# Low bits of the 64-bit weights moved from GpSimd and VectorE to ScalarE, and one VectorE product moved behind a state update

## The chip, the cores and the metric

The kernel runs on one core of a Trainium2 chip. The metric is device time in microseconds (us) of that core. The core's engines each work through a queue of their own in order: PE (TensorE, matmuls; PEld is its weight load), DVE (VectorE), ACT (ScalarE), POOL (GpSimd) and SP (SyncE, which issues the transfers here).

## The reference

Three stages follow each other: a chunked state-space attention, a dense feed-forward network, and a mixture of eight experts. Cut to what matters:

```python
# 1. attention: x (4,8,768,32), a (4,8,768), B and C (4,8,768,16), float32; chunks of 32
cum = cumsum(log(clip(a)))                       # per chunk
M   = (C @ B.T) * exp(cum_i - cum_j) * causal
y   = M @ x + (C @ state) * exp(cum)             # C times decay
state = exp(sum(la)) * state + B.T @ (x * exp(cum_last - cum))
# 2. dense: 3072 tokens, 256 -> 2048 -> 256; w_in and w_out are drawn as float64
h = x @ w_in;  x = maximum(0.01 * h, h) @ w_out
# 3. experts: argmax of x @ w_gate + modality_bias[modality_id], then
out[mask] = gate * (relu(x[mask] @ w1[e]) @ w2[e])
```

`w_in` and `w_out` reach the chip as 64-bit words (1,048,576 of them, two 32-bit halves each) and are turned into float32 there.

## The kernel before, in words

Tokens go in chunks of 128 (24 chunks; six to a batch row) and in six blocks of 512. Attention fills a block's four chunks into `xh` and `xl`, the high and low float32r parts of x. The dense stage then loops over 16 slices of d_ff for each block: `mm1(j, f)` makes `h` in six matmuls, ACT scales it (`sa`), DVE takes the maximum (`gg`), ACT rounds it (`gh`), DVE subtracts (`gl`), and `mm2(j, f)` uses `gh` and `gl` in six matmuls. Attention of the next block runs between these matmuls. Experts come last.

The first four chunks and the first four weight pieces run in an order written out by hand (`STAGED`, L981 to L997). Everything else is placed by the framework's planner, which simulates the run and puts an instruction into an engine's queue when its operands are ready by its own estimate; it may do so between two staged steps. Operations named in `pin` stay behind the engine's instruction that was traced before them; a manual dependency does so for one instruction.

The names that the change and the prediction touch:

- Weight pieces. Each of the 16 pieces (128x512 words) passes through `cv_hb`, `cv_lb`, `cv_or`, a rounding copy to `wih` or `woh` on ACT and a subtraction to `wil` or `wol` on POOL. `i0`, `i1`, `o0`, `o1` are the staged pieces; `hb` and `lb` have two buffers each; `raw` has three.
- `attn_cd(c)` makes `cd` = C times decay on DVE (not for the first chunk of a batch row, so not for 0, 6, 12, 18). `cd` has two buffers. `tr_d(c)` transposes it on PE and so frees its buffer; `tr_c(c)` makes `cm`.
- `p3_mm(c)` multiplies with the state `st` and fills `psy`; `p3_x(c)` evicts it into `xh` (ACT) and `xl` (DVE); `p3_st(c)` updates `st` on DVE. `mm1(0, 0)` needs `xl` of chunk 3.
- `attn_load(c)` issues four transfers on SP: `ct`, `bt`, `xt` and, from chunk 4 on, the broadcast `e` of 512 KB.

The staged end of chunk 3 reads: `(p3_mm, 3), (p3_x, 3), (orr, "o0"), (p3_st, 3), (cast, "o0"), (hb, "o1", 0, 1), (lb, "o1"), (sub, "o0"), (orr, "o1")`.

Of the kernel before, what the change touches and what calls it, by code (L numbers as in the profile page):

```python
# [11 lines left out]
I32 = mybir.dt.int32  # L12
U16 = mybir.dt.uint16
AF = mybir.ActivationFunctionType
ALU = mybir.AluOpType
# [2 lines left out]
PSUM = bass.MemoryType.PSUM  # L18
DRAM = bass.MemoryType.DRAM
NEG = -1.0e30  # L20
LOW, LOW0 = 0.9 * 2.0 ** -13, 0.2995
WHY = "the table is built on the chip from counts and clamped to this range"

# [65 lines left out]
def kernel(  # L89
# [70 lines left out]
    v, s, g, t_ = Pinned(nc.vector, "v"), Pinned(nc.scalar, "s"), Pinned(nc.gpsimd, "g"), Pinned(nc.tensor, "t")  # L160
# [49 lines left out]
    dfull = cst.tile([P, NB, NCB], F32, name="dfull")  # L210
    st = cst.tile([P, P], F32, name="st")
# [89 lines left out]
    dk = {}  # L301
# [62 lines left out]
    def attn_load(c, bcast=True):  # L364
# [10 lines left out]
            nc.sync.dma_start(out=e, in_=cumd[b * H:(b + 1) * H, sl].unsqueeze(0).to_broadcast([P, H, P]))  # L375
        ch[c] = dict(x=xt, b=bt, c=ct, e=e)

    def attn_mask(c):
        e = ch[c]["e"]
        r = g.affine_select(out=e, in_=e, pattern=[[0, H], [1, P]], compare_op=ALU.is_ge, fill=NEG, base=0, channel_multiplier=-1)  # L380
        if c == NC0:
            tc.add_manual_dep(
                r.ins, dk["last"].ins.name, mybir.DependencyInfo(mybir.DependencyClass.NoSync, mybir.DependencyReason.DATA),
                reason="behind the first chunks and conversions in the queue: it waits for a transfer",
            )

    def attn_cd(c):
        b, cc = divmod(c, NCB)
        if cc == 0:
            return  # L390
        d = ch[c]
        cd = ap_.tile([P, H, N], F32, tag="cd", name="cd")
        v.tensor_tensor(
            out=cd, in0=d["c"], in1=ecum[:, cc, b * H:(b + 1) * H].unsqueeze(2).to_broadcast([P, H, N]), op=ALU.mult
        )
        d["cd"] = cd

    def attn_exp(c, h0, h1, src=None):
# [141 lines left out]
    def p3_st(c):  # L540
        b, cc = divmod(c, NCB)
        ps = ch.pop(c)["psy"]
        if cc < NCB - 1:
            gmv = gm.rearrange("p (u a) d -> p u a d", a=2)
            bx = ps[:, 2 * P:2 * P + 64].rearrange("p (a d) -> p a d", a=2).unsqueeze(1).to_broadcast([P, 2, 2, D])
            pm = st if cc == 0 else ap_.tile([P, P], F32, tag="pm", name="pm")
            r = v.tensor_tensor(out=pm.rearrange("p (u a d) -> p u a d", u=2, a=2), in0=bx, in1=gmv, op=ALU.mult)
            readers.append(r)
            if cc > 0:
                v.scalar_tensor_tensor(out=st, in0=st, scalar=dfull[:, b, cc:cc + 1], in1=pm, op0=ALU.mult, op1=ALU.add)  # L550


    def split(raw, hi, lo, eng):
# [11 lines left out]

    def cv_lb(raw, hb, lb):
        w4 = raw.bitcast(U16).rearrange("p (f w) -> p f w", w=4)
        g.tensor_scalar(out=lb, in0=w4[:, :, 3], scalar1=32768.0, scalar2=-(2.0 ** 31), op0=ALU.is_ge, op1=ALU.mult)

    def cv_or(raw, hb, lb):  # L570
        w4 = raw.bitcast(U16).rearrange("p (f w) -> p f w", w=4)
        l2 = lb.bitcast(U16).rearrange("p (f w) -> p f w", w=2)
        v.tensor_scalar(out=l2[:, :, 0], in0=w4[:, :, 1], scalar1=LOW, scalar2=LOW0, op0=ALU.mult, op1=ALU.add)
        hi = hb.bitcast(I32)
        v.scalar_tensor_tensor(out=hi, in0=hi, scalar=3, in1=lb, op0=ALU.logical_shift_left, op1=ALU.bitwise_or)

    def to_f32(raw, q):
        c = cv_hb(raw)
        cv_lb(*c)
        cv_or(*c)  # L580
        return c[1]
# [348 lines left out]
    def p3(c):  # L930
        p3_mm(c)
        p3_x(c)
        p3_st(c)
# [7 lines left out]
    NC0 = blocks[0][1] // P  # L941
# [23 lines left out]
    def lb(key):  # L965
        if W64:
            cv_lb(*cvs[key][1])

    def orr(key):
        if W64:  # L970
            cv_or(*cvs[key][1])
# [5 lines left out]
    def sub(key):  # L977
# [3 lines left out]
    STAGED = [  # L981
        (decay_a,), (tr_mm, 0), (bc_mm, 0, 0), (bc_mm, 0, 1), (decay_b,), (tr_c, 0), (tr_b, 0), (decay_rows,),
        (bc_exp, 0, 0), (bc_mask, 0, 0), (bc_exp, 0, 1), (bc_mask, 0, 1), (cb_mm, 0), (decay_high,), (attn_cd, 1),
        (hb, "i0", 0, 0), (lb, "i0"), (decay_low_s,), (cb_bs, 0), (cb_mul, 0, 0), (cb_mul, 0, 1), (decay_low_v,),
        (cb_mul, 0, 2), (cb_mul, 0, 3), (decay_out,), (warm, 1, 6), (tr_mm, 1), (tr_d, 1), (tr_c, 1), (tr_b, 1), (tr_de, 1),
        (bc_mm, 1, 0), (bc_mm, 1, 1), (bc_exp, 1, 0), (bc_mask, 1, 0), (bc_exp, 1, 1), (bc_mask, 1, 1),
        (p3_mm, 0), (orr, "i0"), (p3_x, 0), (p3_st, 0), (decay_full_mm,), (decay_full,), (cb_mm, 1), (warm, 2, 4),
        (hb, "i1", 0, 1), (cast, "i0"), (cb_bs, 1), (cb_mul, 1, 0), (cb_mul, 1, 1), (attn_cd, 2), (cb_mul, 1, 2),
        (cb_mul, 1, 3), (lb, "i1"), (tr_mm, 2), (tr_d, 2), (tr_c, 2), (tr_b, 2), (tr_de, 2), (orr, "i1"), (attn_cd, 3),
        (bc_mm, 2, 0), (bc_mm, 2, 1), (bc_exp, 2, 0), (bc_mask, 2, 0), (bc_exp, 2, 1), (bc_mask, 2, 1),  # L990
        (p3_mm, 1), (p3_x, 1), (cast, "i1"), (sub, "i0"), (p3_st, 1), (cb_mm, 2), (cb_bs, 2),
        (cb_mul, 2, 0), (cb_mul, 2, 1), (cb_mul, 2, 2), (cb_mul, 2, 3), (tr_mm, 3), (tr_d, 3), (tr_c, 3), (tr_b, 3), (tr_de, 3),
        (bc_mm, 3, 0), (bc_mm, 3, 1), (bc_exp, 3, 0), (bc_mask, 3, 0), (bc_exp, 3, 1), (bc_mask, 3, 1),
# [28 lines left out]
    for c in range(NC0, NCH):  # L1022
        j, col = chunk_block(c)
        o = NF * (j - 1) + NF * col // blocks[j][1] + (Q["sh1"] if j == 1 else Q["sh"])
        if c > NC0 + 1:
            at(o - Q["ld"], attn_load, c)
        if col == 0:
            at(o - 1, new_xt, j)
        at(o - Q["cd"], attn_cd, c)
        at(o - Q["mk"], attn_mask, c)  # L1030
        at(o - Q["tr"], attn_tr, c)
        at(o - Q["ea"], attn_exp, c, 0, 4)
        at(o - Q["eb"], attn_exp, c, 4, 8)
        at(o - Q["c0"], attn_cb, c)
        at(o + Q["p3"], p3, c)
# [109 lines left out]
```

## Time and profile before

| | |
|---|---|
| median of 3 runs | 553.29 us (551.73 to 555.44) |
| profiled execution | 550.48 us, span 548.8 us |
| mean granted clock of PE | 0.967 |
| busy PE, DVE, ACT, POOL | 507.1, 350.2, 312.1, 196.9 us |

Times in the rows are counted from the start of the span. A granted clock of 1.00 is 2.4 GHz and 0.50 is 1.2 GHz. In timeline rows, brackets hold the idle time of the engine ahead of the instruction and what ended it. All helper calls have line L153, so tiles tell the rows apart.

### The profile page before, as it was taken

Reading aid. Unit: us, or ns where it says so; the run is one execution under the profiler, and the core shown is the slowest. Engines: PE = TensorE matmul, PEld = TensorE weight load, DVE = VectorE, ACT = ScalarE, POOL = GpSimd, SP = SyncE. Lnnn points to the kernel's source line nnn. Section 1 sums busy time; section 2 is a strip of 40 time slices with the busy share of each in tenths; the row PEclk is TensorE's granted clock in tenths of the full one; section 3 lists DMA queues with packets and bytes.
Section 4 is the critical chain, followed back from the end, with each engine's and each line's share of the span. In section 5 each row is a group of like instructions: output and inputs, shape, how many; then the busy total and the mean of one; then the engine's idle time right before and its main releaser. Section 6 shows DMA issues by size and latency. Waiting matters only on the chain.

```text
span 548.8 us, 9656 instructions
## 1 busy us (share of the span) xinstructions
PE 507.1 (92%) x3501; PEld 413.9 (75%) x3501; DVE 350.2 (64%) x729; ACT 312.1 (57%) x651; POOL 196.9 (36%) x167
## 2 busy tenths in 40 slices
PE   8857798899999999999999999999989999999991
PEld 5525476577777777677767877788879999999990
DVE  5746897866657675676657676766586665555640
ACT  5523868665555665565566646463536665566640
POOL 5557799310311012100310020073063456656331
PEclk9967989899999999999999999999989999999996
DMA  8895570431235221722060056642169767777400
GB/s 202 144 255 121 139 205 7 92 78 11 53 54 108 54 58 7 150 58 59 4 143 1 2 15 139 194 139 22 59 195 152 232 194 223 240 228 239 132 19 23
DMA packets 128311, 61.01 MB, mean 111 GB/s; under 512 B 84545, under 2 KB 120514, under 8 KB 128258
## 3 DMA queue, kind: packets, MB, share of 16 engines
q1 hardware_dynamic: 125186, 53.94, 42.4%
q0 software_dynamic: 3072, 6.41, 3.6%
q8 instruction: 29, 0.48, 0.4%
q14 instruction: 24, 0.20, 0.1%
HBM read 53.73 MB, written 6.60 MB: 110 GB/s over the span
## 4 chain that ended last, share of the span: by engine, by line
PE 58%; ACT 3%; issue 2%; DVE 2%; POOL 1%; POOLq 0%; DVEq 0%
PE y L153 16%; PE h L153 15%; PE hp L153 12%; PE o L153 10%; PE psy L153 2%; ACT e L153 1%; PE xps L153 1%; PE yr L153 1%; PE ps L153 1%; PE cb L153 1%; POOL out_dram L153 1%; DVE w2s L153 1%; ACT cdt L153 1%; PE lp L153 1%; DVE gg L153 0%
## 5 line engine op out<-in xcount | busy, mean ns | idle before, releaser
L153 ACT CAST gh<-gg 128x512 fp32r<-128x512 f32 x96 | 59.5, 620 | 73.4 <-DVE gg L153 72.0
L153 DVE TENSOR_TENSOR gl<-gg,gh 128x512 fp32r<-128x512 f32 x96 | 73.0, 761 | 32.7 <-ACT gh L153 31.3
L153 POOL TENSOR_SCALAR_AFFINE_SELECT e<-e 128x1024 f32<-128x1024 f32 (+1 forms) x28 | 29.1, 1045 | 171.0 <-DMA e<-cumd 55.9
L153 PE MATMUL h<-xh,wih 128*128 128x512 f32 x192 | 80.3, 423 | 6.6 <-DVE gg L153 5.0
L153 PE MATMUL h<-xl,wih 128*128 128x512 f32 x192 | 77.4, 403 | 5.6 <-DVE xl L153 5.6
L153 DVE TENSOR_TENSOR gg<-sa,h 128x512 f32<-128x512 f32 x96 | 65.6, 684 | 24.8 <-ACT sa L153 23.0
L153 PE MATMUL y<-gl,woh 128*128 128x512 f32 x192 | 76.7, 402 | 0.7 <-DVE gl L153 0.6
L153 PE MATMUL h<-xh,wil 128*128 128x512 f32 x192 | 76.2, 400 | 0.0
L153 ACT ACTIVATE sa<-h 128x512 f32<-128x512 f32 x96 | 56.9, 593 | 32.4 <-PE h L153 32.1
L153 PE MATMUL y<-gh,wol 128*128 128x512 f32 x192 | 75.0, 393 | 0.0
L153 PE MATMUL hp<-x2h,w1s 128*128 128x256 f32 x384 | 72.6, 285 | 0.0
L153 PE MATMUL o<-w2s,hh 128*128 128x256 f32 x384 | 69.3, 285 | 0.0
L153 PE MATMUL y<-gh,woh 128*128 128x512 f32 x192 | 66.7, 406 | 1.0 <-ACT gh L153 1.0
L153 DVE SCALAR_TENSOR_TENSOR hl<-hp,hh 128x512 fp32r<-128x512 f32 x48 | 33.0, 692 | 53.6 <-ACT hh L153 53.4
L153 PEld LDWEIGHTS hp<-x2h,w1s 128*128 128x128 f32 x384 | 61.8, 194 | 0.6
L153 PEld LDWEIGHTS o<-w2s,hh 128*128 128x128 f32 x384 | 58.4, 191 | 0.4 <-issue 0.4
L153 POOL TENSOR_TENSOR w2s<-r,w2s 128x1024 fp32r<-128x1024 f32 x12 | 33.4, 2785 | 65.4 <-ACT w2s L153 40.6
L153 PE MATMUL hp<-x2l,w1s 128*128 128x256 f32 x192 | 53.8, 286 | 0.0
L153 PEld LDWEIGHTS h<-xh,wih 128*128 128x128 f32 x192 | 36.7, 193 | 20.9 <-DVE gg L153 9.1
L153 ACT ACTIVATE hh<-hp 128x512 fp32r<-128x512 f32 x48 | 28.5, 597 | 40.6 <-PE hp L153 40.6
L153 ACT ACTIVATE e<-e,ncum 128x128 f32<-128x128 f32 x160 | 51.2, 395 | 0.0
L153 PE MATMUL o<-w2s,hl 128*128 128x256 f32 x192 | 51.1, 283 | 0.0
(192 smaller groups left out, 916.3 us busy)
## 6 DMA issues: line engine op xcount, KB each, us to landing
r<-in_moe_w_dram SPq DMA_DIRECT2D x48, 512.0 KB, 4.9
e<-cumd SPq DMA_DIRECT2D x20, 512.0 KB, 4.6
raw<-in_moe_w_in_dram SPq DMA_DIRECT2D x4, 1024.0 KB, 5.7
raw<-in_moe_w_out_dram SPq DMA_DIRECT2D x4, 1024.0 KB, 7.3
yx<-ysb SPq DMA_DIRECT2D x6, 528.0 KB, 3.3
xt<-in_x_dram SPq DMA_DIRECT2D x24, 128.0 KB, 4.4
ct<-in_C_dram SPq DMA_DIRECT2D x24, 64.0 KB, 3.1
bt<-in_B_dram SPq DMA_DIRECT2D x24, 64.0 KB, 2.7
```

The lines of the kernel that those rows point to most:

```text
L153: r = f(*args, **kw)
```

## The change

Two edits. First, the low 32-bit half: ScalarE now computes it (scale and bias on the low half's upper 16 bits, written as whole 32-bit words), where GpSimd wrote the sign bit as a word and VectorE then wrote the scaled low bits into that word's lower half. VectorE then joins in two steps: shift `hb` and or it with `lb`, as before; then take the sign bit from `raw` and or it in. No GpSimd instruction is left in `cv_lb`. Second, `cd` of chunk 4 (`NC0`) gets a manual dependency on the state update of the last staged chunk, 3, so that it stands behind it in DVE's queue.

```diff
+SIGN = -(2 ** 31)
...
+    def after(r, key):
+        tc.add_manual_dep(
+            r.ins, dk[key].ins.name, mybir.DependencyInfo(mybir.DependencyClass.NoSync, mybir.DependencyReason.DATA),
...
         if c == NC0:
+            after(r, "last")
...
     def attn_cd(c):
...
-        v.tensor_tensor(
+        r = v.tensor_tensor(
             out=cd, in0=d["c"], in1=ecum[:, cc, b * H:(b + 1) * H].unsqueeze(2).to_broadcast([P, H, N]), op=ALU.mult
         )
+        if c == NC0:
+            after(r, "lastv")
...
-                v.scalar_tensor_tensor(out=st, in0=st, scalar=dfull[:, b, cc:cc + 1], in1=pm, op0=ALU.mult, op1=ALU.add)
+                dk["lastv"] = v.scalar_tensor_tensor(out=st, in0=st, scalar=dfull[:, b, cc:cc + 1], in1=pm, op0=ALU.mult, op1=ALU.add)
...
     def cv_lb(raw, hb, lb):
         w4 = raw.bitcast(U16).rearrange("p (f w) -> p f w", w=4)
-        g.tensor_scalar(out=lb, in0=w4[:, :, 3], scalar1=32768.0, scalar2=-(2.0 ** 31), op0=ALU.is_ge, op1=ALU.mult)
+        s.activation(out=lb, in_=w4[:, :, 1], func=AF.Copy, scale=LOW, bias=LOW0)

     def cv_or(raw, hb, lb):
-        w4 = raw.bitcast(U16).rearrange("p (f w) -> p f w", w=4)
-        l2 = lb.bitcast(U16).rearrange("p (f w) -> p f w", w=2)
-        v.tensor_scalar(out=l2[:, :, 0], in0=w4[:, :, 1], scalar1=LOW, scalar2=LOW0, op0=ALU.mult, op1=ALU.add)
+        w = raw.bitcast(I32).rearrange("p (f w) -> p f w", w=2)
         hi = hb.bitcast(I32)
         v.scalar_tensor_tensor(out=hi, in0=hi, scalar=3, in1=lb, op0=ALU.logical_shift_left, op1=ALU.bitwise_or)
+        v.scalar_tensor_tensor(out=hi, in0=w[:, :, 1], scalar=SIGN, in1=hi, op0=ALU.bitwise_and, op1=ALU.bitwise_or)
```

The mask of chunk 4 kept its dependency on `last`; it now goes through the helper `after`.

## Rows read from the trace of the kernel before

**Rows 1.** Windows: span, PE, PEld, DVE, ACT, POOL busy, PEclk, DMA share, GB/s.

```profile
30.00:40.00 10.00, 6.11 (x63) 3.41 (x62) 4.27 (x11) 3.87 (x11) 7.16 (x6) 0.55 1.00 291
...
70.00:80.00 10.00, 9.99 (x54) 7.45 (x52) 10.00 (x20) 5.79 (x13) 9.62 (x6) 0.91 0.68 173
...
180.00:220.00 40.00, 40.00 (x251) 31.06 (x249) 26.07 (x62) 23.08 (x55) 6.42 (x6) 1.00 0.20 33
```

**Rows 2.** Timeline of PE at the first slice: start, duration, instruction, idle before.

```profile
38.22 1.22 PE L153 MATMUL h<-xh,wih 128*128 128x512 f32 x2 [0.51 <-ACT xh L153]
45.08 0.80 PE L153 MATMUL h<-xl,wih 128*128 128x512 f32 x1 [5.63 <-DVE xl L153]
```

**Rows 3.** Timeline of DVE, 24 to 51 us.

```profile
26.46 0.29 DVE L153 TENSOR_TENSOR cd<-ct,ecum 128x128 f32<-128x128 f32 x1 [2.36 <-DMA ct<-in_C_dram]
...
30.05 0.28 DVE L153 TENSOR_TENSOR cd<-ct,ecum 128x128 f32<-128x128 f32 x1
...
44.39 0.29 DVE L153 TENSOR_TENSOR cd<-ct,ecum 128x128 f32<-128x128 f32 x1 [8.12 <-DMA ct<-in_C_dram]
44.60 0.42 DVE L153 TENSOR_TENSOR xl<-psy,xh 128x256 fp32r<-128x256 f32 x1
...
48.24 0.69 DVE L153 TENSOR_TENSOR gg<-sa,h 128x512 f32<-128x512 f32 x1
49.62 1.06 DVE L153 TENSOR_TENSOR gl<-gg,gh 128x512 fp32r<-128x512 f32 x1 [0.69 <-ACT gh L153]
```

**Rows 4.** Timeline of PE: the transpose that reads chunk 4's `cd`.

```profile
35.31 0.42 PE L153 MATMUL ps<-ident,cd 128*128 128x128 f32 x1
```

**Rows 5.** Timeline of SP, 23 to 42 us.

```profile
23.50 0.38 SPq L371 DMA_DIRECT2D ct<-in_C_dram  x1
...
25.50 0.38 SPq L371 DMA_DIRECT2D ct<-in_C_dram  x1
...
29.60 7.59 SPq L375 DMA_DIRECT2D e<-cumd  x3
...
40.82 1.57 SPq L371 DMA_DIRECT2D ct<-in_C_dram  x1
```

**Rows 6.** Groups by shape, 13 to 110 us: busy, mean ns, idle before, releasers.

```profile
L153 POOL TENSOR_SCALAR lb<-raw 128x512 int32<-128x512 uint16 x16 | 33.3, 2080 | 6.0 <-DVE hb L153 6.0
L153 DVE SCALAR_TENSOR_TENSOR hb<-hb,lb 128x512 int32<-128x512 int32 x16 | 12.9, 807 | 2.6 <-ACT hb L153 2.2
L153 ACT ACTIVATE hb<-raw 128x512 f32<-128x512 f32 x16 | 10.8, 678 | 0.0
L153 DVE TENSOR_SCALAR lb<-raw 128x512 uint16<-128x512 uint16 x16 | 9.2, 572 | 0.0
```

**Rows 7.** Waits between 24 and 110 us: total, times, longest.

```profile
PE h L153 <- DVE gg L153: 4.8, 4, 2.4
...
PEld psy L153 <- POOL lb L153: 1.3, 1, 1.3
```

**Rows 8.** Timeline of ACT ahead of the longest of those waits.

```profile
66.50 0.65 ACT L153 ACTIVATE hb<-raw 128x512 f32<-128x512 f32 x1
67.04 0.59 ACT L153 ACTIVATE sa<-h 128x512 f32<-128x512 f32 x1
```

**Rows 9.** Timeline of POOL and DVE where they run side by side.

```profile
56.97 1.29 POOL L153 TENSOR_TENSOR wil<-hb,wih 128x512 fp32r<-128x512 f32 x1
57.43 1.37 DVE L153 SCALAR_TENSOR_TENSOR hb<-hb,lb 128x512 int32<-128x512 int32 x1
...
81.97 2.38 POOL L153 TENSOR_SCALAR lb<-raw 128x512 int32<-128x512 uint16 x1
...
83.46 0.69 DVE L153 SCALAR_TENSOR_TENSOR hb<-hb,lb 128x512 int32<-128x512 int32 x1
```

**Rows 10.** Timeline of ACT and DVE around the first piece.

```profile
13.99 0.62 ACT L153 CAST cumb<-cr 64x512 bf16<-64x512 f32 x1 [0.17 <-DVE cr L153]
...
15.38 0.68 DVE L153 TENSOR_TENSOR cumb<-cr,cumb 32x512 bf16<-32x512 f32 x1
```

More of the change, by code (lines that the diff above doesn't have):

```diff
@@ L376, in attn_load @@
         ch[c] = dict(x=xt, b=bt, c=ct, e=e)
+    def after(r, key):
+        tc.add_manual_dep(
+            r.ins, dk[key].ins.name, mybir.DependencyInfo(mybir.DependencyClass.NoSync, mybir.DependencyReason.DATA),
+            reason="behind the first chunks in the queue: it waits for a transfer",
+        )
     def attn_mask(c):
@@ L381, in attn_mask @@
         if c == NC0:
[L382 to L385, printed above, removed]
+            after(r, "last")
     def attn_cd(c):
```

## The prediction

> **What bounds the kernel now.** I read the windows first. In the middle of the span PE has no idle time at all: 40.00 of 40.00 us between 180 and 220, at the full clock [rows 1]. Time can be won only where PE waits, and the change touches nothing behind some 105 us. So I looked at the start, and there the window from 30 to 40 us stands out: PE is busy 6.11 of 10 us, and its granted clock is 0.55, so even its busy time is mostly at the 1.2 GHz level. VectorE and ScalarE are idle for more than half of it, while the DMA share is 1.00 [rows 1].
>
> The PE timeline names the loss. The first two matmuls of the dense stage run at 38.22, the third follows after 5.63 us of idle time that `xl` ended [rows 2]. The DVE timeline says why: `xl` stands right behind a `cd` that waited 8.12 us for a `ct` transfer. An earlier `cd` waited 2.36 us for the same kind of transfer [rows 3]; in the staged order `xl` and the state update of chunk 1 come next.
>
> Which chunks are these? The timeline doesn't say, so I counted. `cd` is not made for chunk 6, and the three before 26 us are those of chunks 1 to 3, by their place in the staged order. So 26.46 is chunk 4, 30.05 is chunk 5, and the long wait at 44.39 is chunk **7**, not the chunk that the change moves. It could stand there only because a buffer was free: there are two, and PE read chunk 4's at 35.31 [rows 4], before chunk 7's product was made.
>
> **The change part by part: the moved product.** Behind chunk 3's state update, chunk 4's `cd` can no longer hold `xl` of chunk 1; up to 2.36 us go there. What matters more: chunk 7's `cd` needs the buffer that chunk 4's frees, so it now also comes behind that update, and thus behind `xl` of chunk 3. The edit removes both waits from ahead of the first slice.
>
> What is late next? Chunk 7's `ct` itself. It is issued at 40.82, behind three broadcast loads that keep SP for 7.59 us [rows 5] while the DMA share is 1.00 [rows 1]. The change takes nothing out of that queue, so I leave the arrival at 44.39. The question is what stands behind chunk 7's `cd` when DVE reaches it. PE can transpose chunk 4's product only after it is made, so the earliest place is about when the first `gg` is made. The first free stretch on DVE there is the 0.69 us in which `gl` waits for `gh` [rows 3], and a product whose operands the planner takes as landed fits in. Then DVE waits until 44.39, works 0.29, and the first `gl` starts at 44.68 in place of 49.62: **4.9 us** earlier. The matmuls of two slices, the joins of `o0` and `o1`, and the first `gg` lie in the time that was idle.
>
> The bounds: if the product is put ahead of the second join and of `gg`, these run behind it, 44.68 + 2 x 0.69 + 0.69 + 0.69 = 47.44, and 2.2 us are left. If it comes so late that the transfer has landed, the slice starts at 38.22 - 2.36 = 35.86; from `xl` at 44.60 to `gl` at 49.62 it took 5.02; with 0.4 for the eviction and 0.24 for the longer join `gl` starts at 41.5, a gain of 8.1.
>
> **The low bits.** GpSimd loses 16 x 2.08 = 33.3 us [rows 6]. I price this at nothing: in that group it was GpSimd that waited for VectorE, 6.0 us. One weight load of PE, 1.3 us, is put down to `lb` [rows 7]; it loads a product of chunk 3's `e`, which `lb` doesn't write, so I take that for a wait on VectorE's `e`, and the bound for what goes with it is those 1.3 us.
>
> ScalarE gains 16 instructions. Nothing in the trace reads 16-bit words into a word on ScalarE; the nearest row is `hb`, the same strided source and the same 512 results, 0.678 [rows 6]. Three pieces come before 46 us and fall beside idle time. The tightest is the first: the added instruction pushes the low-part copy at 13.99 by some 0.54, but that ended at 14.61 and was used only at 15.38 [rows 10]; the cover is 0.77, and past it the whole first chunk chain would move. Of the 13 others, all could be hidden (0), or each could push the next instruction by the 0.54 that lie between the starts of `hb` and `sa` at 66.50 [rows 8]: 7.0 us. PE waits four times for `gg`, 4.8 us in all [rows 7], and the longest of these follows that very pair. I take two of thirteen as seen: **1.1 us**.
>
> VectorE trades a 0.572 step for a second join. It has two inputs like the first, one of them strided, so I price it by the first: 0.807 on average, 0.235 more [rows 6], 3.1 us for 13 pieces. The bounds are 0 and that. From 70 to 80 us DVE was busy 10.00 and PE 9.99 [rows 1]: both full, so some of it must show. I take a third: **1.0 us**. The raw tile is also held until the second join, by at most two joins, 1.6 us; SP's next weight load starts that much later. I charge nothing: no wait for a weight load was among those that held PE.
>
> Does GpSimd's absence speed VectorE up? A join beside a GpSimd subtraction took 1.37, but one that ran inside a GpSimd `lb` took 0.69, as if alone [rows 9]. The Trainium skill, page SBUF — State Buffer, section Who interferes with whom, says that a VectorE instruction with two SBUF inputs contends with a GpSimd instruction that reads SBUF and that the loser blocks for the whole instruction. The subtraction's rows agree with it, `lb`'s row does not; by the page the joins would get faster and the sum 0.6 better.
>
> Sum: -4.9 + 1.1 + 1.0 = **-2.8 us**. Against the profiled execution's own 550.48 us that is 547.7. It lies 2.8 below the median of the runs shown, 553.29, and outside their spread, so the prediction is made against the median: **550.5 us**, 0.5% faster.
>
> **The rivals.**
> - The wait goes altogether: chunk 7's product is placed past 44.39. For it: nothing forces it early, and DVE has much queued there. Against: it was placed as early as its buffer allowed before. -8.1 + 2.1 = -6.0: 547.3.
> - The wait moves and keeps its price: chunk 7's product stands ahead of the second join and of `gg`. -2.2 + 2.1: 553.2.
> - The edit doesn't do what it says at chunk 1: chunk 5's `cd` takes chunk 4's old place. Its `ct` is issued 2.0 us later [rows 5], so the wait would grow by 2.0 and all that follows with it. The slice then starts at 40.2 and `gl` at 45.9, a gain of 3.8 less 2.1: 551.6. Against it: in the trace chunk 5's came only 3.6 us later, at a place of its own.
> - Slower: **ScalarE becomes the bound**. It must give `sa` and `gh` in every slice, and 13 more instructions arrive in the same 58 us. From the point where it has no idle time left ahead of `sa`, every one delays a slice: 7.0, and 3.1 of VectorE in full, less 4.9, is +5.2: 558.5. For it: rows 8. Against it: ScalarE was busy only 5.79 of 10 us from 70 to 80 [rows 1].
> - VectorE is freed from GpSimd: the joins fall from 0.807 to 0.69, 1.9 us over 16; a third of it shows: 549.9. This is the page's rule; the row inside `lb` speaks against it.
>
> **How the numbers follow.** Forecast 35%; wait gone 25%; wait moved 17%; chunk 5 in the old place 8%; ScalarE the bound 10%; VectorE freed 5%. About 1% (5.5 us) is what a measurement of this kernel can tell from no change. Faster by more than that, below 547.8, are most of the second case and the lower edge of the first: 0.28. Slower by more, above 558.8, is somewhat under half of the ScalarE case and a planner's order that I don't foresee: 0.08. The rest is 0.64. The range goes from the wait gone with no added cost, 553.29 - 8.1 = 545.2, to the wait that kept its price with half of ScalarE's 7.0 and all of VectorE's 3.1: 553.29 - 2.2 + 6.6 = 557.7.
>
> **What the profile will show.** Right: no `cd` ahead of `xl` of chunks 1 and 3; the 5.63 us of PE gone; a DVE wait for `ct` that still ends near 44.4, with `gl` right behind it; ACT's `lb` near 0.68 and the second join near 0.69 to 0.81; PE waits for `gg` between 50 and 105 us grown by about two. Wrong: the DVE wait ends with another instruction behind it than I say, or is not there; the waits for `gg` grow by more than five; or blocks after 105 us take another time than before, since the planner orders the whole kernel anew.

## The result and the profile after

The changed kernel takes 560.41 us (median of 4 runs, 558.10 to 562.12) beside 552.51 for the kernel before on the same chip: ratio 1.0126, 95% interval 1.0085 to 1.0168. Slower, and outside the predicted range of 545.2 to 557.7. The profiled execution took 559.24, span 557.3, granted clock 0.961.

PE is busy as long as before, 507.4 us against 507.1, so 8.2 of the 8.5 us of longer span are idle time of PE. The windows of the changed kernel show where (span, PE, PEld, DVE, ACT, POOL, PEclk, DMA share, GB/s; they answer to [rows 1]):

```profile
30.00:40.00 10.00, 1.09 (x2) 0.37 (x2) 0.00 (x0) 0.00 (x0) 2.65 (x3) 0.50 1.04 275
...
70.00:80.00 10.00, 7.33 (x43) 4.74 (x43) 6.97 (x18) 8.30 (x18) 4.15 (x5) 1.00 0.49 121
180.00:220.00 40.00, 40.00 (x254) 30.48 (x253) 28.80 (x69) 23.79 (x57) 7.20 (x7) 1.00 0.31 60
```

From 30 to 40 us the core all but stands still: PE is busy 1.09 of 10 us, GpSimd 2.65, DVE and ACT not at all, while the transfers run. The middle of the kernel is full, as before. Summed over windows, PE is idle 6.8 us ahead of 30 us (before 7.0), 13.2 from 30 to 48 (before 9.0), 11.8 from 48 to 110 (before 8.9) and 3.0 from 110 to 360 (before 2.0).

The timeline of PE in the changed kernel, which answers to [rows 2]:

```profile
43.74 1.08 PE L154 MATMUL psy<-e,xt 128*32 128x128 f32 x16 [12.65 <-DVE e L154]
...
45.55 1.22 PE L154 MATMUL h<-xh,wih 128*128 128x512 f32 x2 [0.51 <-ACT xh L154]
46.57 0.63 PE L154 MATMUL h<-xl,wih 128*128 128x512 f32 x1
```

The 5.63 us ahead of the `xl` matmul are gone, as forecast. But PE now waits 12.65 us, and not in the dense stage: it waits for chunk 3's `e`, one step of the attention earlier. The timeline of DVE (answers to [rows 3]):

```profile
28.74 0.42 DVE L154 TENSOR_TENSOR xl<-psy,xh 128x256 fp32r<-128x256 f32 x1 [2.16 <-ACT xh L154]
40.74 1.34 DVE L154 TENSOR_TENSOR bs<-bt,e 128x128 f32<-128x128 f32 x1 [10.99 <-POOL e L154]
45.53 0.42 DVE L154 TENSOR_TENSOR xl<-psy,xh 128x256 fp32r<-128x256 f32 x1 [1.93 <-ACT xh L154]
47.78 0.28 DVE L154 TENSOR_TENSOR cd<-ct,ecum 128x128 f32<-128x128 f32 x1
...
51.17 0.28 DVE L154 TENSOR_TENSOR cd<-ct,ecum 128x128 f32<-128x128 f32 x1
51.37 0.68 DVE L154 TENSOR_TENSOR gl<-gg,gh 128x512 fp32r<-128x512 f32 x1
```

No `cd` waits for `ct` any more. DVE waits 10.99 us for a mask from GpSimd, chunk 3's, and the first `gl` starts at 51.37 in place of 49.62. A mask (`AFFINE_SELECT`) overwrites the part of a chunk's `e` on one side of the diagonal; it stands between the making of `e` and its use. Chunks 0 to 3 get their `e` from ACT, the later ones from a broadcast transfer. So the next view is GpSimd's timeline:

```profile
36.58 1.09 POOL L154 TENSOR_SCALAR_AFFINE_SELECT e<-e 128x1024 f32<-128x1024 f32 x1 [12.21 <-DMA e<-cumd]
38.44 2.26 POOL L154 TENSOR_SCALAR_AFFINE_SELECT e<-e 128x1024 f32<-128x1024 f32 x3 [0.76 <-DMA e<-cumd]
40.67 1.26 POOL L154 TENSOR_TENSOR wil<-hb,wih 128x512 fp32r<-128x512 f32 x1
```

GpSimd waited 12.21 us for a broadcast transfer before it masked a chunk with it. That first mask is 128x1024, a whole chunk; a staged chunk is masked in two instructions of 128x512. The second row groups three masks of two shapes. Which chunks? The order of GpSimd's instructions in the built program tells them by buffer number (`e_197` is chunk 2's, `e_204` chunk 3's; `e_613`, `e_680`, `e_862` are those of chunks 5, 6, 7). Before, and then changed:

```
AFFINE_SELECT e_197<-e_197 128x512 x2
TENSOR_TENSOR wil_138<-hb_313,wih_137 128x512
AFFINE_SELECT e_204<-e_204 128x512 x2
...
AFFINE_SELECT e_613<-e_613 128x1024

AFFINE_SELECT e_197<-e_197 128x512 x2
TENSOR_TENSOR wil_138<-hb_313,wih_137 128x512
AFFINE_SELECT e_613<-e_613 128x1024
AFFINE_SELECT e_680<-e_680 128x1024
AFFINE_SELECT e_204<-e_204 128x512 x2
```

The planner put the masks of chunks 5 and 6 ahead of chunk 3's last two. Chunk 4's mask has a manual dependency on `last`; those of 5 and 6 have none. GpSimd ran them in that order: chunk 3's masks, whose operand came from ACT, which had no work from 30 to 40 us, waited behind two that needed a 512 KB transfer each. One wait has gone out of DVE's queue, and another, longer one stands in GpSimd's. The waits between 24 and 110 us (total, times, longest) show it passed on, and answer to [rows 7]:

```profile
POOL e L154 <- DMA e<-cumd: 19.8, 5, 12.2
...
PE psy L154 <- DVE e L154: 12.7, 1, 12.7
DVE bs L154 <- POOL e L154: 11.0, 1, 11.0
...
PE h L154 <- DVE gg L154: 6.4, 4, 3.0
DVE hb L154 <- ACT lb L154: 5.8, 5, 3.0
```

The groups by shape, 13 to 110 us (busy, mean ns, idle before and its releaser), answer to [rows 6]; the two joins are told apart by their operands, `hb<-hb,lb` the first and `hb<-raw,hb` the second:

```profile
L154 DVE SCALAR_TENSOR_TENSOR hb<-raw,hb 128x512 int32<-128x512 int32 x16 | 13.4, 839 | 0.2
L154 DVE SCALAR_TENSOR_TENSOR hb<-hb,lb 128x512 int32<-128x512 int32 x16 | 11.6, 725 | 5.8 <-ACT lb L154 5.8
...
L154 ACT ACTIVATE lb<-raw 128x512 int32<-128x512 uint16 x15 | 9.9, 672 | 0.0
```

### The profile page after: what moved, and what is told of

Same layout as the page of the kernel before. It is cut to its first block, busy times and chain, and to the rows that moved or that the text cites. A ratio compares the mean times of both kernels' runs of the same rounds, so it can differ in the third digit from the quotient of the medians.

```text
span 557.3 us, 9643 instructions
## 1 busy us (share of the span) xinstructions
PE 507.4 (91%) x3501; PEld 412.6 (74%) x3501; DVE 350.3 (63%) x729; ACT 320.5 (58%) x667; POOL 165.7 (30%) x151
## 4 chain that ended last, share of the span: by engine, by line
PE 73%; DVE 9%; ACT 7%; issue 4%; DMA 2%; POOL 2%; SPq 1%; POOLq 0%; DVEq 0%; ACTq 0%
PE y L154 21%; PE h L154 21%; PE hp L154 11%; PE o L154 10%; PE psy L154 4%; ACT e L154 2%; DVE hb L154 2%; PE cb L154 2%; DMA e<-cumd 1%; PE ps L154 1%; DVE e L154 1%; PE yr L154 1%; ACT lb L154 1%; DVE gg L154 1%; PE xps L154 1%
```

## The experiments

Theory (the "queue theory" of the expectations): the loss is the order of GpSimd's queue. Rivals: the moved product makes it; ScalarE's added work makes it; GpSimd, emptied, let the masks forward; the second join costs by itself. Each run is compared with the kernel before on the same chip.

**e1: hold the masks of chunks 5 to 7 behind chunk 3's.** All of the change stays.

```diff
         if c == NC0:
             after(r, "last")
+        elif c < NC0 + 4:
+            after(r, "lastm")
...
-        g.affine_select(
+        dk["lastm"] = g.affine_select(
```

> The changed kernel with one more hold: the masks of chunks 5 to 7 stand behind the last staged mask of chunk 3 in GpSimd's queue. Queue theory (most of the loss is the GpSimd queue, where two masks that wait for transfers stand ahead of chunk 3's mask): GpSimd no longer waits ahead of chunk 3's mask, the first slice starts near 36 us in place of 45.6, the first gl near 44.7 to 46 in place of 51.4, and the time falls by 4 to 6 us, to 554 to 556. ScalarE theory (the loss is the 16 added ScalarE instructions): the time stays at 559 to 561, and PE waits for gh, gl and gg after 48 us stay. Moved-product theory (the new place of chunk 4's product is itself the loss): stays at 559 to 561.

Measured: 553.15 us, ratio 1.0025 (0.9999 to 1.0051). Of the loss, 7.3 us come back by the medians, 5.6 by the ratios; the queue theory said 4 to 6. In the built program GpSimd's queue is the only one that differs from the changed kernel's, and only in where those masks stand. DVE's timeline:

```profile
37.47 0.42 DVE L154 TENSOR_TENSOR xl<-psy,xh 128x256 fp32r<-128x256 f32 x1 [1.94 <-ACT xh L154]
...
43.79 1.30 DVE L154 TENSOR_TENSOR cd<-ct,ecum 128x128 f32<-128x128 f32 x1
45.01 0.68 DVE L154 TENSOR_TENSOR gl<-gg,gh 128x512 fp32r<-128x512 f32 x1
```

`xl` of chunk 3 starts 8.1 us earlier than in the changed kernel and the first `gl` 6.4. The wait in GpSimd's queue is the main cause. But `gl` is also 4.6 earlier than before the change, and yet the time is that of before: something gives it back later. Up to ACT's copy of the sixth dense block's result, where both have run the same 2312 matmuls, PE was idle 25.6 us in e1 and 26.7 before, and busy 367.0 and 364.6.

**e2: the moved product alone**, on the kernel before, bits untouched.

```diff
-        v.tensor_tensor(
+        r = v.tensor_tensor(
             out=cd, in0=d["c"], in1=ecum[:, cc, b * H:(b + 1) * H].unsqueeze(2).to_broadcast([P, H, N]), op=ALU.mult
         )
+        if c == NC0:
+            tc.add_manual_dep(
+                r.ins, dk["lastv"].ins.name, mybir.DependencyInfo(mybir.DependencyClass.NoSync, mybir.DependencyReason.DATA),
...
-                v.scalar_tensor_tensor(out=st, in0=st, scalar=dfull[:, b, cc:cc + 1], in1=pm, op0=ALU.mult, op1=ALU.add)
+                dk["lastv"] = v.scalar_tensor_tensor(out=st, in0=st, scalar=dfull[:, b, cc:cc + 1], in1=pm, op0=ALU.mult, op1=ALU.add)
```

> The kernel before with the moved product alone; the low bits stay on GpSimd and VectorE. Queue theory: GpSimd's order is that of the kernel before, so there is no wait there; both VectorE waits ahead of xl go; 2.2 to 8.1 us faster than before by the bounds of the prediction, 545 to 551, and the first gl at 44.7 to 47.4. ScalarE theory: the same, since nothing is added to ScalarE. Moved-product theory: slower than before, 556 to 561.

Measured: 549.76, ratio 0.9955 (0.9930 to 0.9980). DVE's timeline:

```profile
36.68 0.43 DVE L153 TENSOR_TENSOR xl<-psy,xh 128x256 fp32r<-128x256 f32 x1 [1.93 <-ACT xh L153]
...
43.56 1.09 DVE L153 TENSOR_TENSOR gl<-gg,gh 128x512 fp32r<-128x512 f32 x1 [0.69 <-ACT gh L153]
44.58 0.71 DVE L153 TENSOR_TENSOR cd<-ct,ecum 128x128 f32<-128x128 f32 x1
```

The moved product is a gain, so the rival that blames it falls. `gl` starts 6.1 us earlier than in [rows 3], and chunk 7's `cd` stands behind it with nothing to wait for. Only some 2.5 of the 6.1 reach the end; the busy times of its profile show one reason:

```profile
PE 510.1 (93%) x3501; PEld 414.5 (76%) x3501; DVE 354.3 (65%) x729; ACT 312.2 (57%) x651; POOL 196.0 (36%) x167
```

The span of this execution is 548.0, so PE is idle 37.9 us in place of 41.7; but the same 3501 matmuls are busy 3.0 us longer. The windows of e2 show more work where the granted clock is low:

```profile
30.00:48.00 18.00, 14.09 (x70) 9.26 (x67) 13.86 (x24) 7.17 (x16) 13.50 (x11) 0.65 0.96 219
```

Before, PE was busy 9.04 us in that stretch, at a clock of 0.53. A mean of 0.65 is part 1.2 and part 2.4 GHz, and PE had been waiting ahead of it. Matmuls moved there from later stretches at nearly full clock are busy longer; that the 3.0 us come from them is how I read it and wasn't tried by itself. It is a reading of one execution of each kernel: over all runs beside e2 the median granted clock was 0.960 before and 0.967 in e2, the other way round than in these two (0.967 and 0.962). So why 2.5 us and not 6.1 reach the median stays open in part. From 48 to 110 us PE is idle 10.0 us in place of 8.9.

**e3: the bits alone** (the changed kernel without the dependency of chunk 4's `cd`).

```diff
-        if c == NC0:
-            after(r, "lastv")
```

> The changed kernel without the hold on chunk 4's product. Queue theory: the wait on GpSimd stays, and VectorE waits for ct ahead of xl come back as well, partly beside it: 559 to 563. ScalarE theory: the added instructions cost the same as in the changed kernel: 559 to 561. Moved-product theory: back to the kernel before, 552 to 554.

Measured: 558.34, ratio 1.0109 (1.0061 to 1.0157). GpSimd waits 8.2 us for the broadcast and DVE 5.7 for GpSimd. The loss belongs to the edit of the bits; beside its wait, the moved product makes no difference that can be told (1.0109 without it, 1.0126 with it).

**e4: the low bits on GpSimd**, as whole words, the two joins kept.

```diff
-        s.activation(out=lb, in_=w4[:, :, 1], func=AF.Copy, scale=LOW, bias=LOW0)
+        g.tensor_scalar(out=lb, in0=w4[:, :, 1], scalar1=LOW, scalar2=LOW0, op0=ALU.mult, op1=ALU.add)
```

> The changed kernel with the low bits as whole words on GpSimd in place of ScalarE; the two joins on VectorE and the moved product stay. The masks of chunks 5 and 6 still stand ahead of chunk 3's in its queue. Queue theory: the first slice still starts near 45 us; with the ScalarE part (about 3 us of PE waits after 48 us) gone the time is 556 to 559, and with none of it gone 559 to 561. ScalarE theory (all of the loss): 552 to 554.

Measured: 557.93, ratio 1.0105 (1.0061 to 1.0150). GpSimd has its 16 instructions again and ScalarE none of the added ones, yet the masks of chunks 5 and 6 stand ahead as in the changed kernel: GpSimd waits 8.9 us, DVE 7.6. So neither the emptied GpSimd nor ScalarE turns the order over. What is left that e3, e4 and the changed kernel share is the pair of joins.

**f1: e1 with the low bits on GpSimd** (the edit of e4 on e1).

> As e1 (masks of chunks 5 to 7 behind chunk 3's, moved product, two joins), but the low bits are made by GpSimd as whole words (multiply and add, 0.97 us each in e4) and not by ScalarE (0.66 each in e1). It takes 16 of some 0.66 us from ScalarE and leaves the second join. If ScalarE's added work is what puts e1 (553.15) behind the product alone (549.76): 549 to 550.5, and the waits of TensorE for gh in the weight stretch gone back. If it is the second join on VectorE: about 553, as e1, with TensorE's wait for gg at 7 us or so. If GpSimd's own time at 48 to 60 us decides (11.69 of 12 us busy with the product alone): under 549.

Measured: 555.73, ratio 1.0062 (1.0040 to 1.0084). The ScalarE theory wanted 549 to 550.5; f1 is 2.0 us slower than e1 by the ratios, 2.6 by the medians, and outside all three expectations. In DVE's timeline chunk 7's `cd`, which stands ahead of the first `gl` in e1 too, waits again:

```profile
34.75 0.42 DVE L154 TENSOR_TENSOR xl<-psy,xh 128x256 fp32r<-128x256 f32 x1 [1.93 <-ACT xh L154]
...
44.79 0.29 DVE L154 TENSOR_TENSOR cd<-ct,ecum 128x128 f32<-128x128 f32 x1 [3.22 <-DMA ct<-in_C_dram]
45.00 1.77 DVE L154 TENSOR_TENSOR gl<-gg,gh 128x512 fp32r<-128x512 f32 x1
```

`xl` of chunk 3 is 2.7 us earlier here than in e1, and the wait uses that lead up: the first `gl` starts when e1's does. So the wait doesn't set f1 apart from e1. The profile is also of the fastest of the seven runs (553.08). The reason wasn't found.

**f2: an idle ScalarE activation for each piece**, on e2, masks held; its result is read by nothing.

```diff
+        idle = ap_.tile([P, 512], I32, tag="idle", name="idle")
+        s.activation(out=idle, in_=w4[:, :, 1], func=AF.Copy, scale=LOW, bias=LOW0)
```

> The product alone, with the low bits on GpSimd as before and one join, and for each of the 16 pieces one more ScalarE activation of the same size whose result nobody reads (16 of some 0.66 us). If ScalarE's added work is what e1 loses against the product alone: about 553. If it isn't: 549.5 to 550.3, as the product alone (549.76).

Measured: 551.90, ratio 0.9991 (0.9964 to 1.0017), 2.1 over e2, between what the two theories said. Twelve of the activations between 48 and 110 us took 0.674 us each. This is what the added work costs if nothing is taken away elsewhere.

**f3 and f3b: a second join for each piece**, on e2, masks held; the 16-bit step stays, the sign is set twice. The same kernel ran twice; the rows below are of the second run.

```diff
         v.scalar_tensor_tensor(out=hi, in0=hi, scalar=3, in1=lb, op0=ALU.logical_shift_left, op1=ALU.bitwise_or)
+        v.scalar_tensor_tensor(out=hi, in0=w[:, :, 1], scalar=-(2 ** 31), in1=hi, op0=ALU.bitwise_and, op1=ALU.bitwise_or)
```

> The product alone, with the low bits on GpSimd as before, and for each of the 16 pieces a second join on VectorE that sets the sign bit once more (16 of some 0.7 us). If the second join is what e1 loses against the product alone: 552 to 553.5, with TensorE's wait for gg longer than with the product alone. If it isn't: 549.5 to 550.3.

> The kernel of f3 once more, for a profile at the clock of the other runs. If the second join is what costs: again 556 to 559, with VectorE busier between 48 and 110 us than with the product alone and TensorE idle there for 14 us or more, against 10.0. If f3's time came from something else: nearer 550, or the idle time in another stretch.

Measured: 558.49, ratio 1.0096 (1.0060 to 1.0133), and 558.86, ratio 1.0132 (1.0090 to 1.0174): 7.8 to 9.8 us over e2 by the ratios. That is three times what the join theory said for f3 (2.2 to 3.7 over e2); f3b's expectation, written after f3, came true. The windows from 48 to 110 us, f3b first, then e2:

```profile
48.00:110.00 62.00, 47.72 (x251) 32.68 (x252) 59.31 (x97) 40.51 (x95) 48.04 (x28) 0.91 0.41 105
```

```profile
48.00:110.00 62.00, 51.99 (x292) 35.10 (x292) 53.69 (x96) 44.45 (x108) 46.71 (x29) 0.92 0.46 118
```

With the join, DVE is busy 59.31 of 62 us, all but full, and PE is idle 14.3 against 10.0.

**g1: the sign word as a float times zero on GpSimd**, on e2, masks held; one join.

```diff
-        g.tensor_scalar(out=lb, in0=w4[:, :, 3], scalar1=32768.0, scalar2=-(2.0 ** 31), op0=ALU.is_ge, op1=ALU.mult)
+        g.tensor_scalar(out=lb.bitcast(F32), in0=w[:, :, 1], scalar1=0.0, scalar2=None, op0=ALU.mult)
```

> The product alone with the masks held, and GpSimd's sign word made by one multiplication (upper word as a float times zero, which leaves only the sign) in place of the comparison and multiplication of 2.08 us. One join, the 16-bit step and ScalarE as in the kernel before. If the form of the operation sets GpSimd's time, as the low bits of e4 (0.97) say, the sign word takes about 1.0 us and GpSimd is no longer full from 48 to 60 us: 546 to 548.5, and the idle time of TensorE from 48 to 110 us under the 10.0 of the product alone. If GpSimd's fullness was not on the path: 549.5 to 550.

Measured: 550.44 beside 553.19, ratio 0.9946 (0.9917 to 0.9975); e2 had 0.9955, so no difference that can be told. The sign word took 1.70 us, not 1.0, and PE was idle 10.2 us from 48 to 110. A miss: this form of the sign word isn't the fast one that was expected, and whether GpSimd's fullness is on the path stays open.

**g2: the sign word by ScalarE**, as times zero with -0.0 added, on e2, masks held; one join, the 16-bit step on DVE. The weights came out without their sign, so the experts get other tokens, with more blocks of work (3601 weight loads in place of 3501). The time at the end, 575.66 (ratio 1.0431, 1.0389 to 1.0473), tells nothing; up to the last dense block the work is the same in kind and count.

```diff
-        g.tensor_scalar(out=lb, in0=w4[:, :, 3], scalar1=32768.0, scalar2=-(2.0 ** 31), op0=ALU.is_ge, op1=ALU.mult)
+        s.activation(out=lb.bitcast(F32), in_=w[:, :, 1], func=AF.Copy, scale=0.0, bias=-0.0)
```

> The product alone with the masks held, and the sign word by ScalarE (upper word as a float times zero), nothing by GpSimd: ScalarE's 16 added activations and GpSimd's emptied queue as in e1, but one join and the 16-bit step in place of two joins. If the second join is what holds e1 back (553.15): 547 to 549.5. If ScalarE's added work is: 552 to 553, as e1 and the idle activation (551.9).

Measured by ACT's copy of the sixth dense block's result: 390.71 us, against 392.55 in e1 and 389.22 in e2. These are single executions, 1.8 and 1.5 us apart, which is too little to decide; it leans to the join as what holds e1 back.

**h1: the changed kernel without its second join**, nothing held. It leaves the sign of the weights out, so again only the time up to the sixth block counts (at the end 574.13, ratio 1.0404, 1.0336 to 1.0471, from two runs, 575.90 and 572.36; the profile is of the first).

```diff
         v.scalar_tensor_tensor(out=hi, in0=hi, scalar=3, in1=lb, op0=ALU.logical_shift_left, op1=ALU.bitwise_or)
-        v.scalar_tensor_tensor(out=hi, in0=w[:, :, 1], scalar=SIGN, in1=hi, op0=ALU.bitwise_and, op1=ALU.bitwise_or)
```

> The changed kernel without its second join and with nothing else: the sign of the weights is left out, so the experts get other tokens and the time behind some 390 us can't be compared; what counts is the time up to the last copy of a dense block's result. In every program built so far with two joins a piece, the planner puts the masks of chunks 5 and 6 ahead of chunk 3's last staged masks on GpSimd; in those with one join it puts them behind, and so in this one. If the second join is what turns the order over: no wait of GpSimd near 12 us, the split of chunk 3 on VectorE near 37 us in place of 45.53, the first gl near 45 in place of 51.37, and the sixth block's first copy near 391 in place of 399.48. If the emptied GpSimd queue or ScalarE's work makes the loss: GpSimd's wait and 399 stay.

Measured. GpSimd's timeline, and DVE's:

```profile
27.99 1.22 POOL L154 TENSOR_SCALAR_AFFINE_SELECT e<-e 128x512 f32<-128x512 f32 x2 [3.64 <-ACT e L154]
...
39.96 1.34 POOL L154 TENSOR_SCALAR_AFFINE_SELECT e<-e 128x1024 f32<-128x1024 f32 x1 [9.52 <-DMA e<-cumd]
```

```profile
34.24 0.42 DVE L154 TENSOR_TENSOR xl<-psy,xh 128x256 fp32r<-128x256 f32 x1 [1.93 <-ACT xh L154]
...
39.65 0.69 DVE L154 TENSOR_TENSOR gl<-gg,gh 128x512 fp32r<-128x512 f32 x1 [0.69 <-ACT gh L154]
45.33 0.82 DVE L154 TENSOR_TENSOR cd<-ct,ecum 128x128 f32<-128x128 f32 x1 [4.98 <-DMA ct<-in_C_dram]
```

Chunk 3's two masks run at 27.99, ahead of the broadcast masks. GpSimd still waits 9.52 us for a transfer, but behind them, where chunk 3 doesn't need it. With the second join goes the order, though GpSimd is as empty and ScalarE as loaded as in the changed kernel. ACT's copies of the sixth block's result in the changed kernel, in e1 and in h1, each from its timeline of ACT:

```profile
399.48 0.59 ACT L154 COPY yt<-y 128x512 f32<-128x512 f32 x1 [0.79 <-PE y L154]
```

```profile
392.55 0.59 ACT L154 COPY yt<-y 128x512 f32<-128x512 f32 x1 [0.79 <-PE y L154]
```

```profile
389.05 0.59 ACT L154 COPY yt<-y 128x512 f32<-128x512 f32 x1 [0.79 <-PE y L154]
```

So the second join costs 10.4 us up to there (changed kernel to h1). With it gone, h1 stands where e2 does, 389.22. By these rows 6.9 of the 10.4 are the order (changed kernel to e1) and 3.5 the join itself (e1 to h1), but each row is of one execution, and e1's was late ahead of anything that its edit moves. Chunk 2's masks in the changed kernel, in e1 and in h1:

```profile
21.92 1.22 POOL L154 TENSOR_SCALAR_AFFINE_SELECT e<-e 128x512 f32<-128x512 f32 x2 [3.77 <-ACT e L154]
```

```profile
24.70 1.23 POOL L154 TENSOR_SCALAR_AFFINE_SELECT e<-e 128x512 f32<-128x512 f32 x2 [5.13 <-ACT e L154]
```

```profile
21.89 1.22 POOL L154 TENSOR_SCALAR_AFFINE_SELECT e<-e 128x512 f32<-128x512 f32 x2 [3.76 <-ACT e L154]
```

The windows from 20 to 24 us of the changed kernel and of e1, whose queues are the same up to there:

```profile
20.00:24.00 4.00, 3.97 (x57) 2.67 (x55) 3.36 (x8) 2.55 (x7) 2.08 (x3) 1.00 1.07 273
```

```profile
20.00:24.00 4.00, 4.00 (x17) 2.04 (x15) 2.77 (x8) 1.40 (x5) 0.00 (x0) 0.50 0.90 166
```

Counted from chunk 2's masks, the order takes 9.7 us and the join itself 0.7; e1's runs give the order 5.6 to 7.3. So the order is the larger part, and what the join costs by itself here, some 1 to 5 us, isn't settled.

**h2: e2 with the second join and the masks not held** (the added line of f3 on the kernel of e2). GpSimd's instructions, the 16-bit step and ScalarE are as before the change.

> The product alone and a second join a piece, as in f3, but without the hold on the masks, so that the planner puts the masks of chunks 5 and 6 ahead of chunk 3's last two, though all 16 low-bit instructions of GpSimd, the 16-bit step and ScalarE are as before the change. If the second join's order makes the wait: VectorE waits some 5 us or more for GpSimd's mask ahead of chunk 3's bs, and the time is 4 to 8 us over f3 (558.5, 558.9), so 562.5 to 567. If the wait needs GpSimd emptied or the low bits on ScalarE: about 558.5, as f3.

Measured: 562.91, ratio 1.0204 (1.0150 to 1.0257), at the lower end of what the order theory wanted, and 4.0 to 6.0 us over f3b and f3 by the ratios. DVE's timeline:

```profile
40.41 1.34 DVE L153 TENSOR_TENSOR bs<-bt,e 128x128 f32<-128x128 f32 x1 [7.94 <-POOL e L153]
45.20 0.42 DVE L153 TENSOR_TENSOR xl<-psy,xh 128x256 fp32r<-128x256 f32 x1 [1.93 <-ACT xh L153]
```

GpSimd's timeline has the whole-chunk masks ahead, as in the changed kernel:

```profile
36.27 1.09 POOL L153 TENSOR_SCALAR_AFFINE_SELECT e<-e 128x1024 f32<-128x1024 f32 x1 [9.17 <-DMA e<-cumd]
```

The second join alone makes the wait.

## Why the prediction was wrong, point by point

**What bounds the kernel**: right. The loss and the gain both lie where PE waits ahead of 110 us, first of all from 30 to 48.

**The moved product**: right in place, too large at the end. Forecast, the first `gl` 4.9 us earlier with chunk 7's `cd` ahead of it and still waiting; in e2 it came 6.1 earlier with the `cd` behind it, which is the rival "the wait goes altogether". In f1 the forecast case itself appeared (3.22 us), in h1 the wait behind the first `gl` (4.98). What reached the end was 2.5 us: a `gl` that starts earlier isn't an end that comes earlier by as much. In the profiled execution PE's matmuls were busy 3.0 us longer and it waited 1.1 us more from 48 to 110. The prediction booked 4.9 at the start as 4.9 at the end.

**The low bits on GpSimd, "I price this at nothing"**: not refuted. The wait stands in GpSimd's queue, but emptying that queue doesn't make it. e4 gives GpSimd its 16 instructions back and has the wait (8.9 us) and the loss (557.93); h1 leaves them out, has no wait ahead of chunk 3's masks, and reaches the sixth block's result at 389.05, e2 at 389.22.

**VectorE, 1.0 us**: this is the step that failed. The term prices the second join by its length on DVE and takes the order of the other queues as it was: what the join does to GpSimd's order is put at nothing, and no reason is given. For the moved product I walked the order of DVE's queue past every chunk; for the bits I priced durations. An order that wasn't foreseen is named only among the chances, as a part of 0.08. What the runs show in place of 1.0 us is 10.4 us up to the sixth block (changed kernel to h1), of which the order of GpSimd's queue is the larger part (5.6 to 7.3 us by e1's runs).

The planner places by its own estimate of when operands are ready, and an instruction that needs a transfer can go ahead of one that the path needs if nothing pins it. The masks of chunks 5 and 6 were free to do so, before the change as well, and that could be read from the code: chunk 4's alone is held. Every kernel here with two joins a piece and no hold (the changed one, e3, e4, h2) has the masks of chunks 5 and 6 ahead of chunk 3's; every one with one join and no hold (before, e2, h1) has them behind. By which of its estimates the planner is turned over wasn't traced: the second join's time on DVE and the raw tile, which is held until that join has read it, were not told apart.

The length itself was priced nearly rightly: the two joins took 0.725 + 0.839 = 1.564, against 0.807 + 0.572 = 1.379 in [rows 6], 0.185 more a piece (forecast 0.235), 3.0 us for 16. What the join costs with the order held is 7.8 to 9.8 us where the 16-bit step stays (f3, f3b). In e1, which has no such step, the whole edit of the bits costs 3.4 us over e2 by the medians.

**ScalarE, 1.1 us**: `lb` took 0.672, as the `hb` row said. Added to e2 alone it costs 2.1 (f2); in h1, where the 16-bit step and GpSimd's work go with it, nothing is left to see. The rival "ScalarE becomes the bound" gave 558.5, near the result by luck: e4 has none of that work and loses nearly as much.

**VectorE freed from GpSimd**: not shown. The first join fell from 0.807 to 0.725 in the changed kernel, towards the 0.69 of the rival, but it took 0.801 in e1 and 0.792 in h1, where GpSimd has as little to do; with the low bits on GpSimd, in e4, it took 0.961 (all means of 16). The Trainium skill, page SBUF — State Buffer, section Who interferes with whom, has a VectorE instruction with two SBUF inputs contend with a GpSimd instruction that reads SBUF. e4's figure is in its direction, e1's and h1's show no gain, and the orders differ between all of these.

**The signs named ahead**: no `cd` ahead of `xl`, the 5.63 us gone, `lb` and the joins near their prices, and PE's waits for `gg` grown by 1.6 us (4.8 to 6.4) were all seen. What showed it wrong was the sign that the DVE wait for `ct` "is not there": another wait, for a mask, is. The later blocks weren't touched: from the third dense block's result to the sixth's it took 166.3 us before and after.

The best versions here are e2 (0.9955) and g1 (0.9946): the moved product alone.

## What to carry to other kernels

Where a planner fills in-order queues, an edit is costed by the order that it leaves in every queue, not by the durations alone: for each queue ask which instructions wait for a transfer, what holds them behind the path, and whether the edit or only its timing can let one forward. An instruction that waits for a transfer, and that only the planner's estimate keeps behind the path, needs a pin: here chunk 4's mask had one, those of chunks 5 to 7 had none. Time that is won at the start of a kernel is checked at a later landmark, such as the first result of a later block, before it is booked at the end. And before two traces are compared at a landmark, look whether they already differ ahead of the edit.

## What the runs showed of the hardware

- On GpSimd, the time of one instruction with 512 results a partition went with the operation and the type of its source. From strided 16-bit words, compare and multiply took 2.08 us [rows 6], multiply and add 0.91 (e4, 16 instructions); one multiplication of strided floats took 1.70 (g1).
- DVE's first join, one instruction of one shape, had a mean from 13 to 110 us of 0.73 us in the changed kernel and of 0.96 in e4.
- Two executions can part ahead of any edit: from 20 to 24 us PE ran 57 matmuls at a granted clock of 1.00 in the changed kernel and 17 at 0.50 in e1, from the same queues.
- PE's matmuls are no fixed cost: the same 3501 were busy 507.1 us in one execution of the kernel before and 510.1 in one of e2.
